# Windowed attention with a gated feed-forward block: the score table added by TensorE in jobs 1 to 12, one reduction for both heads' minima, the first 27 steps' scores in two-bank tiles

## The chip, the cores and the metric

The kernel runs on one core of a Trainium2 chip. Its engines work through queues of their own, each in order: TensorE (PE, with its weight loads shown as PEld), VectorE (DVE), ScalarE (ACT), GpSimd (POOL) and SyncE (SP, which here only issues loads). TensorE writes its results to PSUM, which the program uses as eight banks of 512 fp32 columns; the rest lies in SBUF. The metric is the time of one execution on the device in microseconds, less is better.

## What is computed

Attention over 4 batches, 8 heads, 768 positions and 64 dimensions, where a query sees the last 96 keys and the first 8, with a slope of distance for each head, and then a feed-forward block with a three-tap convolution and a gate:

```python
scores = scale * np.matmul(q, k.transpose(0, 1, 3, 2))
keep = is_global | is_local
slopes = 2.0 ** (-8.0 * (np.arange(H, dtype=np.float32) + 1) / H)
bias = -slopes[:, None, None] * dist[None, :, :]
scores = np.where(keep, scores + bias, -1000000000.0)
a = np.exp(scores - np.max(scores, axis=-1, keepdims=True))
attn = np.matmul(a / (np.sum(a, axis=-1, keepdims=True) + 1e-09), v)
...
h = np.maximum(x @ w_in, 0.0)          # x is attn, heads side by side
conv_out[s] = sum(conv_w[k] * h[s + k - 1] for k in range(3))
out = (h * sigmoid(conv_out)) @ w_out
```

## The kernel before

**Jobs and steps.** A job is one batch, one half of the positions (384) and one pair of heads; there are 32 jobs, numbered m, and each has three steps i of 128 queries. Step s is step i of job m, s = 3m + i, so jobs 1 to 12 are steps 3 to 38. A query block sees a window of 232 key columns (96 before it, its own 128, and 8 global ones); the first block of a batch sees 136.

**What a step does.** `scores` multiplies q by k for both heads into PSUM. In jobs 0 to 8 ("native", `m < NATIVE`) these are plain fp32 matmuls of 64 rows, head 0 in rows 0 to 63 and head 1 in rows 64 to 127 (line 384); head 0's tile is s, head 1's is sb, in different banks. From job 9 on q is split into a high and a low fp32r part (qh, ql) and k is stacked (kk), and each head takes two matmuls (line 394), both heads in one bank. `maxima` is VectorE's: one pass per head over the scores in PSUM adds the bias table `tab` (bf16, a column block per head; masked places hold a huge value), scales by -0.125, writes the result back and keeps the minimum in mm (line 411, in the profile as CUSTOM_DVE_ANT_0 with an accumulator read behind it). `exps` is ScalarE's: exp(minimum - value) for each head into one of three buffers pbuf, with the sum (line 425). `normalise` takes the reciprocal on VectorE (437) and multiplies head 0 on GpSimd (443) and, in the first 40 steps, head 1 on ScalarE (441). Two steps later `transposes` turns both heads on TensorE (451), ScalarE copies them out (453), and at a job's end `values` multiplies by v (469) and `mixed` splits the result into xh and xl (481, 482).

**The feed-forward block.** A half of a batch is four jobs, 12 steps. Then `mm1` (line 500; 521 for the first piece, done early) multiplies by w_in, ScalarE's relu goes to hbuf (510), `conv` runs on GpSimd (546) and VectorE (547, 548), a gate and a check on ScalarE (566, 577), `split` on VectorE and ScalarE (599 to 602), and `mm2` multiplies by w_out (611). These items are spread over the steps of the next half.

**Decode.** The weights arrive as 64-bit floats in 16 pieces (w0_0 to w7_1) and VectorE cuts them into fp32 by three operations a piece (315, 317, 319); GpSimd casts the high plane wih or woh (324) and VectorE subtracts the low plane wil or wol (330). How many such operations are put behind a step's minima is set by budgets in us: `DECODE_BY_HAND` for steps 0 to 10 and `DECODE_LATER` from step 11 on. A piece's load waits until a slot of four is free.

**Loads.** SyncE issues all of them in one order: q and k of a job (rq, rk; line 111 for native jobs, four loads each), v (122) and weight pieces (306). The program lets the issue of a load wait for the landing of the eighth before it. `prep` casts k and q of jobs from 9 on, on GpSimd (136, 137), and VectorE subtracts (140, 141).

**Order.** Steps 0 to 10 stand in the order in which the code is written, with matmuls on zeros (`warm`, 169) between them. From step 11 on a scheduler orders each engine's instructions. PSUM: two buffers of s (a bank each), two of transposes, one of pv, and three others m0 to m2, of which m0 and m1 hold sb up to step 26 and then products of the feed-forward block.

## Time and profile before

| what | us |
|---|---|
| median of three runs | 463.97 |
| lowest and highest of them | 452.75, 464.49 |
| the profiled execution | 452.65 |
| its span, first to last instruction | 450.7 |
| TensorE busy in the span | 434.5 |
| VectorE busy | 351.9 |
| ScalarE busy | 304.0 |
| GpSimd busy | 225.8 |

The busy time of an engine is the union of its instructions; a matmul's end is modelled, so it says when TensorE had something in flight, not that it ran at its peak. A view by windows gives these times for a stretch, with the number of instructions in brackets, TensorE's granted clock (1.00 is 2.4 GHz), and the share of time in which the DMA engines were busy. The chain of waits goes back from the last instruction to what released it, and so on to the start: what stands in it set the time.

### The profile page before, as it was taken

Reading aid. Unit: us, or ns where it says so; the run is one execution under the profiler, and the core shown is the slowest. Engines: PE = TensorE matmul, PEld = TensorE weight load, DVE = VectorE, ACT = ScalarE, POOL = GpSimd, SP = SyncE. Lnnn points to the kernel's source line nnn. Section 1 sums busy time; section 2 is a strip of 40 time slices with the busy share of each in tenths; the row PEclk is TensorE's granted clock in tenths of the full one; section 3 lists DMA queues with packets and bytes.
Section 4 is the critical chain, followed back from the end, with each engine's and each line's share of the span. In section 5 each row is a group of like instructions: output and inputs, shape, how many; then the busy total and the mean of one; then the engine's idle time right before and its main releaser. Section 6 shows DMA issues by size and latency. Waiting matters only on the chain.

```text
span 450.7 us, 9020 instructions
## 1 busy us (share of the span) xinstructions
PE 434.5 (96%) x3027; PEld 375.6 (83%) x3027; DVE 351.9 (78%) x927; ACT 304.0 (67%) x839; POOL 225.8 (50%) x315
## 2 busy tenths in 40 slices
PE   8789999999889999999999999999999999998997
PEld 6555678899768988899989988889989988798876
DVE  6899998889989877757989897847989986447800
ACT  3778878788799667647776576646775696547610
POOL 5654446637835472656675585646675651022000
PEclk9989999999999999999999999999999999999999
DMA  6979941343244332353234333442335223584111
GB/s 213 306 221 275 279 121 43 108 147 105 83 129 150 108 107 97 92 166 107 86 120 160 107 108 91 130 138 81 106 119 163 81 83 119 207 293 132 47 49 52
DMA packets 22662, 60.02 MB, mean 133 GB/s; under 512 B 3024, under 2 KB 5584, under 8 KB 22608
## 3 DMA queue, kind: packets, MB, share of 16 engines
q1 hardware_dynamic: 18992, 53.01, 38.1%
q10 hardware_dynamic: 3616, 6.36, 3.8%
q8 instruction: 26, 0.43, 0.4%
q14 instruction: 28, 0.23, 0.2%
HBM read 53.07 MB, written 6.29 MB: 132 GB/s over the span
## 4 chain that ended last, share of the span: by engine, by line
PE 73%; DVE 5%; ACT 4%; DMA 4%; POOL 2%; issue 2%; ACTq 0%; POOLq 0%; DVEq 0%
PE o L611 24%; PE h L500 24%; PE pv L469 7%; PE t L451 7%; PE s L394 6%; DMA check<-in_w 3%; DVE c L547 1%; PE last L632 1%; POOL pbuf L443 1%; PE sb L384 1%; PE s L384 1%; DVE c L548 1%; DVE c L599 1%; ACT pbuf L425 1%; ACT sat L577 1%
## 5 line engine op out<-in xcount | busy, mean ns | idle before, releaser
L443 POOL TENSOR_SCALAR pbuf<-pbuf,mm 128x232 f32<-128x232 f32 (+1 forms) x152 | 109.1, 726 | 74.1 <-DVE mm L437 49.2
L425 ACT ACTIVATE pbuf<-s,mm 128x232 f32<-128x232 f32 (+1 forms) x165 | 72.5, 444 | 37.6 <-DVE mm L411 22.8
L411 DVE CUSTOM_DVE_ANT_0 s<-s,tab 128x232 f32<-128x232 f32 (+1 forms) x165 | 63.1, 384 | 24.9 <-PE s L394 21.8
L546 POOL TENSOR_SCALAR c<-hbuf,cw 128x382 f32<-128x382 f32 (+1 forms) x64 | 50.0, 786 | 59.3 <-ACT hbuf L510 59.3
L611 PE MATMUL o<-woh,gh 128*128 128x512 f32 x184 | 74.0, 402 | 0.0
L611 PE MATMUL o<-wol,gh 128*128 128x512 f32 x184 | 73.2, 398 | 0.0
L611 PE MATMUL o<-woh,gl 128*128 128x512 f32 x184 | 73.2, 399 | 0.0
L451 PE MATMUL t<-ident,pbuf 128*128 128x128 f32 x384 | 63.0, 278 | 6.6 <-ACT pbuf L441 3.7
L453 ACT ACTIVATE pt<-t 128x512 f32<-128x512 f32 x96 | 58.0, 604 | 15.4 <-PE t L451 15.3
L451 PEld LDWEIGHTS t<-ident,pbuf 128*128 128x128 f32 x384 | 45.5, 141 | 19.6 <-ACT pbuf L441 5.1
L500 PE MATMUL h<-xh,wih 128*128 128x384 f32 x252 | 58.1, 345 | 1.7 <-ACT hbuf L510 1.2
L500 PE MATMUL h<-xl,wih 128*128 128x384 f32 x252 | 58.8, 342 | 0.0
L500 PE MATMUL h<-xh,wil 128*128 128x384 f32 x252 | 56.3, 340 | 0.0
L469 PE MATMUL pv<-pt,v 128*64 128x128 f32 (+1 forms) x768 | 50.0, 279 | 0.3 <-ACT pt L453 0.3
L469 PEld LDWEIGHTS pv<-pt,v 128*64 128x64 f32 (+1 forms) x768 | 42.3, 138 | 8.9 <-issue 2.5
L500 PEld LDWEIGHTS h<-xh,wih 128*128 128x128 f32 x252 | 42.9, 189 | 4.1 <-ACT hbuf L510 1.9
L547 DVE SCALAR_TENSOR_TENSOR c<-hbuf,cw,c 128x382 f32<-128x382 f32 (+1 forms) x64 | 43.7, 697 | 3.0 <-POOL c L546 2.7
L500 PEld LDWEIGHTS h<-xh,wil 128*128 128x128 f32 x252 | 44.2, 189 | 0.3 <-issue 0.3
L500 PEld LDWEIGHTS h<-xl,wih 128*128 128x128 f32 x252 | 44.0, 189 | 0.2 <-issue 0.2
L548 DVE SCALAR_TENSOR_TENSOR c<-hbuf,cw,c 128x382 f32<-128x382 f32 (+1 forms) x64 | 43.4, 686 | 0.3
L510 ACT ACTIVATE hbuf<-h 128x384 f32<-128x384 f32 x64 | 31.9, 500 | 17.4 <-PE h L500 17.0
L611 PEld LDWEIGHTS o<-woh,gl 128*128 128x128 f32 x184 | 34.7, 188 | 7.7 <-issue 0.2
(119 smaller groups left out, 846.6 us busy)
## 6 DMA issues: line engine op xcount, KB each, us to landing
v<-in_vv SPq DMA_DIRECT2D x32, 384.0 KB, 3.7
rq<-in_qk SPq DMA_DIRECT2D x23, 384.0 KB, 3.1
wr<-in_w SPq DMA_DIRECT2D x16, 512.0 KB, 5.2
check<-in_w SPq DMA_DIRECT2D x16, 512.0 KB, 4.6
rk<-in_qk SPq DMA_DIRECT2D x12, 504.0 KB, 3.6
out<-ob ACTq DMA_DIRECT2D x23, 256.0 KB, 2.1
rk<-in_qk SPq DMA_DIRECT2D x11, 408.0 KB, 3.2
rq<-in_qk SPq DMA_DIRECT2D x16, 96.0 KB, 4.4
```

The source lines that it names most:

```text
L411: last_ttr[s] = V.tensor_tensor_reduce(out=sp[j][:, c0 : c0 + n], in0=sp[j][:, c0 : c0 + n], in1=tb, scale=-0.125, scalar=3.0e38, op0=ALU. ...
L425: last_exp[s] = A.activation(pb[:, j, c0 : c0 + n], sp[j][:, c0 : c0 + n], AF.Exp, bias=mm[:, j : j + 1], scale=-1.0, accum_out=mm[:, 2 + ...
L443: G.tensor_scalar(x, x, inv, 1.0, ALU.mult, ALU.mult)
L451: T.transpose(pt[:, j, c, :], pb[:, j, c * P : (c + 1) * P], ident)
L453: last_ev[s] = A.activation(sb, pt, AF.Copy)
L469: T.matmul(pv[m][64 * j : 64 * j + 64, i * P : (i + 1) * P], vt[m][:n, i, c, 64 * j : 64 * j + 64], sb[:n, j, c, :], start=c == 0, stop=c ...
L500: T.matmul(ps[:, :TB], w_[:, k, fs], x_, start=part == 0 and k == 0, stop=part == 2 and k == NK - 1,)
L510: A.activation(half, ps[:, :TB], AF.Relu, scale=0.5)
L546: G.tensor_scalar(c, *tap(1), 1.0, ALU.mult, ALU.mult)
L547: V.scalar_tensor_tensor(c, *tap(0), c, ALU.mult, ALU.add)
L548: V.scalar_tensor_tensor(c, *tap(2), c, ALU.mult, ALU.add)
L611: last = T.matmul(ps, g_[:, f], w_[:, f], start=f == 0 and part == 0, stop=f == NF - 1 and part == 2,)
```

## The change

For jobs 1 to 12 the table is no longer added by VectorE. q is scaled by -0.125 (native jobs: in place, 384 columns, by GpSimd, one multiplication per job, placed where job m - 1 begins; jobs 9 to 12: in the cast and the subtraction that were there). TensorE adds the table with one more matmul per head into the same PSUM columns: the weights are `ident16`, a bf16 identity times -0.125, made once by ScalarE, and the moving data is the table itself, 232 or 136 columns. VectorE then takes the minima of both heads with one `tensor_reduce` and writes nothing back.

For the first 27 steps the scores of both heads lie in one tile of two banks, with two buffers, in place of s and sb. At step 27 this pool is closed, and its four banks become two buffers of s and the banks m0 and m1. The decode budgets are raised. Steps 0 to 2 and 39 to 95 compute as before.

```diff
+BIASED = (1, 13)
-DECODE_BY_HAND, DECODE_LATER = (0.3, 1.2, 1.4), (1.2, 1.2)
+DECODE_BY_HAND, DECODE_LATER = (0.3, 1.5, 1.8), (1.6, 1.6)
...
     def prep(m, part):
+        if m < NATIVE and biased(m) and part == 0:
+            q = raw[m][0][:, :TB]
+            G.tensor_scalar(q, q, -0.125, 1.0, ALU.mult, ALU.mult)
         if m >= len(jobs) or m < NATIVE:
             return
...
-            G.tensor_copy(qh, rq)
+            if biased(m):
+                G.tensor_scalar(qh, rq, -0.125, 1.0, ALU.mult, ALU.mult)
+            else:
+                G.tensor_copy(qh, rq)
...
+            if biased(m):
+                V.scalar_tensor_tensor(ql, rq, -0.125, qh.bitcast(F32), ALU.mult, ALU.subtract)
+            else:
+                V.tensor_tensor(ql, rq, qh.bitcast(F32), ALU.subtract)
...
     table(1, WIN, X=A)
+    A.activation(ident16, ident, AF.Copy, scale=-0.125)
...
-        both = ps_s.tile([P, 2, 256], F32, tag="s", name=f"s{s}")
-        sp = [both[:, 0], bank(f"sb{s}", True) if m < BESIDE else both[:, 1]]
+        if m < BESIDE:
+            both = wide[1].tile([P, 2, 512], F32, tag="s", name=f"s{s}")
+        else:
+            if not ps_s:
+                narrow()
+            both = ps_s[0].tile([P, 2, 256], F32, tag="s", name=f"s{s}", bufs=2)
+        sp = [both[:, 0], both[:, 1]]
+
+        def bias(j):
+            last_mm[s] = T.matmul(
+                sp[j][:, c0 : c0 + n], ident16, bias_of(s, j), start=False, stop=True
+            )
...
+            if biased(m):
+                bias(j)
+        for j in range(2 if m < NATIVE and biased(m) else 0):
+            bias(j)
...
+        if biased(m):
+            last_ttr[s] = V.tensor_reduce(
+                mm[:, 0:2], both[:, :, c0 : c0 + n], axis=mybir.AxisListType.X, op=ALU.min,
+            )
+        for j in range(0 if biased(m) else 2):
             last_ttr[s] = V.tensor_tensor_reduce(
```

What it does to the order is shown in two places. The first is TensorE around steps 15 and 16 (t11 to t13 are transposes of steps 11 to 13, h0_0 the first product of the feed-forward block, pv3 the values of job 3). Before:

```order
L384 MATMUL s15_760<-rk5_585,rq5_586 128x232
L521 MATMUL h0_0_665<-xl1_623,wih_186 128x384
L521 MATMUL h0_0_665<-xh1_622,wil_187 128x384
L384 MATMUL sb15_761<-rk5_585,rq5_586 128x232
L451 MATMUL t11_724<-ident_153,pbuf2_195 128x128 x4
L521 MATMUL h0_0_665<-xh2_717,wih_186 128x384
L384 MATMUL s16_814<-rk5_585,rq5_586 128x232
L451 MATMUL t12_749<-ident_153,pbuf0_193 128x128 x4
L384 MATMUL sb16_815<-rk5_585,rq5_586 128x232
```

And in the changed program:

```order
L417 MATMUL s15_784<-rk5_594,rq5_595 128x232 x2
L409 LDWEIGHTS ident16_158
L409 MATMUL s15_784<-tab_167,ident16_158 128x232
L409 LDWEIGHTS ident16_158
L409 MATMUL s15_784<-tab_167,ident16_158 128x232
L567 MATMUL h0_0_680<-xh2_734,wih_188 128x384
L567 MATMUL h0_0_680<-xl2_735,wih_188 128x384
L567 MATMUL h0_0_680<-xh2_734,wil_189 128x384
```

The two heads' scores, which other work parted before, now stand side by side, with the two additions behind them.

The second place is GpSimd between the normalisations (pbuf) of steps 13 and 16 or 17; c0 is the convolution, woh a cast of weights. Before:

```order
L443 TENSOR_SCALAR pbuf1_194<-pbuf1_194,mm13_711 128x232
L324 CAST woh_188<-w4_1_756 128x512
L443 TENSOR_SCALAR pbuf2_195<-pbuf2_195,mm14_740 128x232
L443 TENSOR_SCALAR pbuf0_193<-pbuf0_193,mm15_764 128x232
L546 TENSOR_SCALAR c0_879<-hbuf_190,cw_185 128x382
L324 CAST woh_188<-w5_0_803 128x512
L443 TENSOR_SCALAR pbuf1_194<-pbuf1_194,mm16_818 128x232
```

And in the changed program:

```order
L489 TENSOR_SCALAR pbuf1_196<-pbuf1_196,mm13_729 128x232
L346 CAST woh_190<-w5_0_749 128x512
L141 TENSOR_SCALAR rq7_831<-rq7_831 128x384
L489 TENSOR_SCALAR pbuf2_197<-pbuf2_197,mm14_758 128x232
L489 TENSOR_SCALAR pbuf0_195<-pbuf0_195,mm15_789 128x232
L592 TENSOR_SCALAR c0_903<-hbuf_192,cw_187 128x382
L141 TENSOR_SCALAR rq8_968<-rq8_968 128x384
L346 CAST woh_190<-w5_1_776 128x512
L346 CAST woh_190<-w6_0_823 128x512
L489 TENSOR_SCALAR pbuf1_196<-pbuf1_196,mm16_843 128x232
```

The casts have moved forward by one or two pieces, and the scaling of q for jobs 7 and 8 stands between the normalisations.

## Rows read from the trace of the kernel before

**Rows 1.** The page's first lines: the span, and TensorE's busy time.

```profile
span 450.7 us, 9020 instructions
...
PE 434.5 (96%) x3027; PEld 375.6 (83%) x3027; DVE 351.9 (78%) x927; ACT 304.0 (67%) x839; POOL 225.8 (50%) x315
```

**Rows 2.** Windows over all engines. After each stretch and its length: PE, PEld, DVE, ACT and POOL busy us with instructions, the granted clock, the DMA engines' busy share, GB/s.

```profile
10.00:35.00 25.00, 20.07 (x175) 14.20 (x175) 23.29 (x84) 18.79 (x65) 15.94 (x23) 0.93 0.89 271
35.00:84.00 49.00, 47.98 (x331) 36.05 (x330) 46.39 (x133) 39.10 (x127) 26.36 (x36) 1.00 0.62 181
84.00:98.00 14.00, 13.53 (x103) 12.44 (x102) 11.21 (x30) 11.56 (x35) 7.32 (x9) 1.00 0.36 122
98.00:140.00 42.00, 38.37 (x286) 33.07 (x285) 38.98 (x84) 35.82 (x101) 23.67 (x24) 1.00 0.34 106
...
200.00:400.00 200.00, 200.00 (x1410) 179.00 (x1407) 157.30 (x404) 133.19 (x354) 108.57 (x143) 1.00 0.39 123
```

**Rows 3.** Pieces of the chain of waits in order of time: start, length, what.

```profile
69.73 2.29 PE h L500 x12
...
100.69 3.13 DMA rq<-in_qk
...
105.69 1.41 POOL pbuf L443
...
118.88 2.61 DVE c L547 x3
...
413.41 22.39 PE o L611 x96
```

**Rows 4.** Windows for line 411 alone (VectorE's minima): its busy time, instructions, clock, DMA share, GB/s.

```profile
10.00:35.00 25.00, 7.28 (x40) 0.93 0.89 271
35.00:84.00 49.00, 13.11 (x60) 1.00 0.62 181
98.00:140.00 42.00, 7.90 (x36) 1.00 0.34 106
```

**Rows 5.** Groups of instructions by line and shape: line, engine, operation, out<-in, count, then busy us, mean ns, idle before. Two shapes of the minima, the subtraction of `mixed`, which reads 384 columns of PSUM, and, from the page, the exponential.

```profile
L411 DVE CUSTOM_DVE_ANT_0 s<-s,tab 128x232 f32<-128x232 f32 x138 | 55.1, 401 | 19.6 <-PE s L394 16.9 <-POOL tab L227 1.2 <-ACT sat L577 0.4
...
L482 DVE TENSOR_TENSOR xl<-pv,xh 128x384 fp32r<-128x384 f32 x32 | 17.6, 551 | 1.6 <-ACT xh L481 1.3
...
L411 DVE CUSTOM_DVE_ANT_0 s<-s,tab 128x136 f32<-128x136 f32 x27 | 8.1, 299 | 5.3 <-PE s L394 4.8 <-PE sb L384 0.3
...
L425 ACT ACTIVATE pbuf<-s,mm 128x232 f32<-128x232 f32 (+1 forms) x165 | 72.5, 444 | 37.6 <-DVE mm L411 22.8
```

**Rows 6.** The timeline of TensorE in the hand-written part, step 5: start, length, operation. Each head's fp32 matmul runs in two parts.

```profile
16.80 0.46 PE L384 MATMUL s<-rk,rq 64*128 64x232 f32 x1
16.81 0.46 PE L384 MATMUL sb<-rk,rq 64*128 64x232 f32 x1
17.11 0.36 PE L384 MATMUL s<-rk,rq 64*128 64x232 f32 x1
...
17.40 0.44 PE L451 MATMUL t<-ident,pbuf 128*128 128x128 f32 x2
```

**Rows 7.** The same timeline in the scheduled part, one step of job 5; x2 are the two parts of one head.

```profile
48.55 0.66 PE L384 MATMUL s<-rk,rq 64*128 64x232 f32 x2
49.14 0.66 PE L451 MATMUL t<-ident,pbuf 128*128 128x128 f32 x4
49.73 0.66 PE L384 MATMUL sb<-rk,rq 64*128 64x232 f32 x2
50.31 0.44 PE L521 MATMUL h<-xh,wih 128*128 128x384 f32 x1
```

**Rows 8.** Windows for line 384 alone (native scores, steps 12 to 26): PE and PEld busy.

```profile
35.00:84.00 49.00, 16.43 (x60) 8.13 (x60) 1.00 0.62 181
```

**Rows 9.** Two pieces of the chain of waits: four score matmuls of 232 columns (two heads, high and low part) of jobs from 9 on, each with its own weights.

```profile
96.08 0.40 PE s L394 x4
...
147.91 0.65 PE s L394 x4
```

**Rows 10.** GpSimd's groups by line and shape: a multiplication by a constant over 368 columns.

```profile
L227 POOL TENSOR_SCALAR tab<-setup 128x368 bf16<-128x368 f32 x6 | 3.8, 649 | 0.2
```

**Rows 11.** The timeline of VectorE: the first decode operation of a piece at two times.

```profile
16.77 0.71 DVE L315 TENSOR_SCALAR w<-wr 128x512 int32<-128x512 int32 x1
...
45.10 0.43 DVE L315 TENSOR_SCALAR w<-wr 128x512 int32<-128x512 int32 x1
```

**Rows 12.** The timeline of GpSimd; in square brackets the idle time before an instruction and what ended it.

```profile
43.85 0.46 POOL L443 TENSOR_SCALAR pbuf<-pbuf,mm 128x232 f32<-128x232 f32 x1
47.72 1.07 POOL L324 CAST woh<-w 128x512 fp32r<-128x512 f32 x1 [3.42 <-DVE w L319]
...
52.50 0.65 POOL L546 TENSOR_SCALAR c<-hbuf,cw 128x382 f32<-128x382 f32 x1 [2.40 <-ACT hbuf L510]
...
54.13 0.63 POOL L443 TENSOR_SCALAR pbuf<-pbuf,mm 128x232 f32<-128x232 f32 x1
```

**Rows 13.** SyncE's timeline at two issues of q loads (the last half of job 7's, both halves of job 8's), and from the view of loads their size and the median time from issue to landing.

```profile
42.92 0.47 SPq L111 DMA_DIRECT2D rq<-in_qk  x1
...
51.98 1.11 SPq L111 DMA_DIRECT2D rq<-in_qk  x2
...
rq<-in_qk SPq DMA_DIRECT2D x16, 96.0 KB, 4.4
```

More of the change, by code (lines that the diff above doesn't have):

```diff
@@ L82, in fast_path, with narrow @@
     pg = pool("pg", 4)
-    ps_s = pool("ps_s", 2, space=PSUM)
     ps_t = pool("ps_t", 2, space=PSUM)
     ps_v = pool("ps_v", 1, space=PSUM)
-    ps_m = pool("ps_m", 1, space=PSUM)
+    ps_m = {2: pool("ps_m", 1, space=PSUM)}
     p2 = pool("p2", 2)
+    ps_w = tc.tile_pool(name="ps_w", bufs=2, space=PSUM)
+    wide = [ps_w, ps_w.__enter__()]
+    ps_s = []
+    def narrow():
+        wide[0].__exit__(None, None, None)
+        ps = tc.tile_pool(name="ps_s", bufs=1, space=PSUM)
+        ps_s.append(ps.__enter__())
+        ps_m[0] = ps_m[1] = ps_s[0]
+        pools.insert(len(pools) - 1, ps)
     jobs = [(b, u, hp) for b in range(B) for u in range(2) for hp in range(NPAIR)]
@@ L123, in load_v, with biased @@
         vt[m] = t
+    def biased(m):
+        return BIASED[0] <= m < BIASED[1]
     def prep(m, part):
+        if m < NATIVE and biased(m) and part == 0:
+            q = raw[m][0][:, :TB]
+            G.tensor_scalar(q, q, -0.125, 1.0, ALU.mult, ALU.mult)
         if m >= len(jobs) or m < NATIVE:
@@ L140, in prep @@
             V.tensor_tensor(kk[64:], rk[64:], kk[64:].bitcast(F32), ALU.subtract)
-            V.tensor_tensor(ql, rq, qh.bitcast(F32), ALU.subtract)
+            if biased(m):
+                V.scalar_tensor_tensor(ql, rq, -0.125, qh.bitcast(F32), ALU.mult, ALU.subtract)
+            else:
+                V.tensor_tensor(ql, rq, qh.bitcast(F32), ALU.subtract)
     manual = tc.manual_schedule()
@@ L151, in fast_path, with bank @@
     load(1)
-    turns = [0, 0]
-    def bank(name, scores=False):
+    turns = [0]
+    def bank(name):
         s = cur.get("s", 0)
         own = (2,) if s < NB * BESIDE else (0,) if exact else (0, 1, 2)
-        if scores:
-            own = (0, 1)
-        turns[scores] += 1
-        k = own[turns[scores] % len(own)]
-        return ps_m.tile([P, 512], F32, tag=f"m{k}", name=name)
+        turns[0] += 1
+        k = own[turns[0] % len(own)]
+        return ps_m[k].tile([P, 512], F32, tag=f"m{k}", name=name)
     queue, cur, exact = [], {}, []
@@ L192, in fast_path @@
     make_identity(nc, ident)
+    ident16 = const.tile([P, P], BF16, name="ident16")
     V.tensor_copy(rel, reli)
@@ L388, in scores @@
                     start=True,
-                    stop=True,
+                    stop=not biased(m),
                 )
@@ L392, in scores @@
             qh, ql, kk = qk[m]
-            for n_, (q_, st, sp_) in enumerate(((qh, True, False), (ql, False, True))):
+            for n_, (q_, st, sp_) in enumerate(((qh, True, False), (ql, False, not biased(m)))):
                 last_mm[s] = T.matmul(
@@ L400, in scores, with bias_of @@
                 )
-        st_s[s] = (sp, c0, n, first)
+            if biased(m):
+                bias(j)
+        for j in range(2 if m < NATIVE and biased(m) else 0):
+            bias(j)
+        st_s[s] = (sp, c0, n, both)
+    def bias_of(s, j):
+        m, i = steps[s]
+        b, u, hp = jobs[m]
+        if u == 0 and i == 0:
+            return tab[:, 2 * hp + j, WIN:]
+        return tab[:, 2 * hp + j, 0:WIN]
     def maxima(s):
@@ L405, in maxima @@
         b, u, hp = jobs[m]
-        sp, c0, n, first = st_s[s]
+        sp, c0, n, both = st_s[s]
         mm = p1.tile([P, 8], F32, tag="mm", name=f"mm{s}", bufs=6)
-        for j in range(2):
-            h = 2 * hp + j
-            tb = tab[:, h, WIN:] if first else tab[:, h, 0:WIN]
+        if biased(m):
[3 more added lines that the diff above has]
+        for j in range(0 if biased(m) else 2):
             last_ttr[s] = V.tensor_tensor_reduce(
-                out=sp[j][:, c0 : c0 + n], in0=sp[j][:, c0 : c0 + n], in1=tb,
+                out=sp[j][:, c0 : c0 + n], in0=sp[j][:, c0 : c0 + n], in1=bias_of(s, j),
                 scale=-0.125, scalar=3.0e38, op0=ALU.add, op1=ALU.min,
@@ L957, in general_head @@
         for c, (a, z) in enumerate(parts):
-            sp = ps_s.tile([P, 512], F32, tag="s", name=f"gs{t}_{c}")
+            sp = ps_s[0].tile([P, 512], F32, tag="s", name=f"gs{t}_{c}", bufs=2)
             T.matmul(
```

## Prediction

> **What bounds the kernel now.** I read the page's summary first, then the windows by stage, then the chain of waits. The summary has a span of 450.7 us, in which TensorE shows as 96% busy [rows 1]; the profiled execution took 452.65 us, so 1.95 us lie around the span. That execution equals the lowest of the three runs shown (452.75) and is 2.4% under their median of 463.97; my sum is made against 452.65, and my time is for an execution like it.
>
> The windows split the span [rows 2]. From 200 to 400 us TensorE is busy without a hole, and the chain there and to the end is made of TensorE's own matmuls, such as the 96 of the output product in one piece of 22.39 us [rows 3]. Nothing of the change touches that part. Ahead of it stand three stages, which I name A (10 to 35 us, steps 3 to 11, by hand), B (35 to 84 us, steps 12 to 26) and C (84 to 140 us, steps 27 to 38). VectorE is busy 23.3 of 25 us in A, 46.4 of 49 in B, 11.2 of 14 and 39.0 of 42 in C; TensorE 20.1, 48.0, 13.5 and 38.4 [rows 2]. So in A VectorE is the tightest, in B both are full, and in C VectorE leads again with ScalarE and GpSimd close by. The chain says the same: TensorE's pieces in B, then at 100 us a load of rq, a multiplication of GpSimd, and convolution steps of VectorE [rows 3]. All 36 changed steps lie in A, B and C, so what is won must be won there, and later stages keep it.
>
> **VectorE: two passes become one.** In B the line of the minima takes 13.11 us for 60 instructions, which is 15 steps of two passes and two accumulator reads: 0.874 us a step; in A it is 0.728 (10 steps, some of them narrow), in C 0.878 [rows 4]. A reduction over 2 x 232 columns of PSUM stands nowhere in the trace. The pass takes 401 ns for 232 columns and 299 ns for 136 [rows 5], so 1.06 ns a column and 155 ns beside it; 464 columns give 647 ns, and 272 give 443 ns. Bounds: not under the 551 ns of the 384-column read of PSUM, which is shorter work [rows 5], and not over two passes, 802 ns. I take 647, since the 384-column row falls on the same line (562 worked out, 551 seen). A wide step so saves 0.23 us (0.07 to 0.32). A and B together have 24 such steps, some narrow in A: 9 x 0.2 + 15 x 0.23 = 5.3 us of VectorE's time. C has 12: 2.7 us.
>
> The larger decode budgets add no work. They bring weight steps forward: by the pass of step 12 five more of them are done, and the last plane of w7_1 comes right ahead of the pass of step 21 or 22 in place of step 27. What A saves on the minima it spends on these, so A alone gets no shorter; B gets it back. I count A and B together for this reason.
>
> **TensorE: the table is added, and split pairs are joined.** In the hand-written part the two heads' scores run beside each other: s and sb start at 16.80 and 16.81, and the transposes follow at 17.40, so 0.60 us for both [rows 6]. In B the scheduler has pulled them apart: s at 48.55, transposes at 49.14, sb at 49.73, the next product at 50.31; each head alone takes the same 0.59 us [rows 7]. The order of the changed program has both heads in one row (x2) in every step of B, then the two additions. By the window, native scores hold TensorE 16.43 us in B, 1.10 us a step [rows 8]; at 0.60 that is 9.0, so 7.4 us go. Each addition is a matmul of 232 columns with its own weight load. The nearest rows are the four 232-column score matmuls of later jobs, 0.40 us in one piece and 0.65 in another, so 0.10 to 0.16 us each [rows 9]. The 30 additions of B cost 3.0 to 4.8 us, and B's net for TensorE is 2.6 to 4.4 us less. In A 18 additions cost 1.8 to 2.9 us; TensorE idles 4.9 us of A and runs warming matmuls besides, which hides them. In C 24 additions cost 2.4 to 3.8 us, with no pair to join; TensorE idles 0.5 + 3.6 us there, which covers them only if they fall into holes. Without that cover C would be up to 3.8 us longer.
>
> **GpSimd: eight more multiplications in its queue.** Jobs 1 to 8 get q scaled in place, 384 columns each; the nearest row is 368 columns at 649 ns [rows 10], so 5.2 us in all. The rows of the trace range either way: VectorE's 512-column bit step takes 0.71 us at 16.77 and 0.43 us at 45.10 [rows 11], so an operation can stretch by 0.28 us, depending on what runs beside it. GpSimd is busy 15.9 of 25 us in A and 26.4 of 49 in B [rows 2], so the time itself fits. What matters is where they stand. GpSimd works in order, and behind a multiplication that waits for its load stand the casts of weights and the normalisations of older steps. Jobs 9 to 12 multiply where they cast, and subtract with a scale where they subtracted: same sizes, no price taken. The scaled identity is one small ScalarE operation ahead of its first exponential, free: ScalarE waits there for the first minimum.
>
> **Waits added.** Scores of a native job now wait for GpSimd besides the load; both stand two steps ahead of their use. The one minimum waits for both heads and the additions, about 0.2 to 0.3 us later, and the first exponential for it; VectorE has decode steps to do meanwhile. Two banks are freed together, after the second exponential in place of the first, so an exponential's 0.44 us later for one head [rows 5].
>
> **The sum.** A and B: VectorE gives 5.3 us, TensorE in B 2.6 to 4.4; since both are full there, the smaller decides, and I take 3.7. C: VectorE gives 2.7, TensorE takes 2.4 to 3.8 in holes of 4.1; I take half of VectorE's, 1.3. Loads, transposes and everything after 140 us: 0. 452.65 - 3.7 - 1.3 = 447.65, say 447.7 us. With the bounds, the gain runs from 0 (each step saves 0.07 us, 1.7 us in A and B, and additions in C take it back) to about 9 (4.4 in B, 1.5 in A, 3 in C), so 443.5 to 452.7.
>
> **Rivals.**
> *Slower: GpSimd is held up at a load.* In the changed order q of job 8 is scaled right behind the first convolution step, ahead of two casts and the normalisation of step 16. Before, that place in the queue was reached at 53.15 (52.50 + 0.65) [rows 12]; the two loads of rq8 were issued in 1.11 us from 51.98 on and such a load lands after 4.4 us [rows 13], so 56.4 to 57.0: 3.2 to 3.8 us with GpSimd idle. For q of job 7 the last load was issued at 42.92, to land at 47.3, and a 512 KB weight load now stands ahead of it, 1.9 us at the 271 GB/s of A [rows 2]: 49.2. The queue is free for it from 44.3 on, but before it waited until 47.72 for a decode step anyway [rows 12], so 1.5 us are new; job 5 the same, 1.5. If all 6.5 us end in transposes that come late, with three buffers between them and the exponentials, A and B lose 6.5 and win nothing, C still wins 1.3: 457.9 us. Against it: the transposes of step 16 stand about two steps (6 us) further back in the changed order. It decides from about 3.7 us of such lateness on, where it eats the gain of A and B.
> *No gain: the loads set the pace.* The DMA engines are 0.89 busy in A [rows 2]. If steps come sooner but loads do not, B begins as before and TensorE waits instead: only C's 1.3 us and a bit, 450.3 to 453.5, middle 452.
> *Multiplications beside decode steps.* Eight more GpSimd operations of 0.65 us each stretch a decode step by between the 0.28 us of [rows 11] and their own length: 2.2 to 5.2 us of VectorE's time in A and B, off the 5.3. Then A and B win between 3.1 and 0.1: 448.3 to 451.3 with C's share, 450 in the middle. The Trainium skill speaks for this one (SBUF — State Buffer, Who interferes with whom): a VectorE instruction with two SBUF inputs contends with a GpSimd instruction that reads SBUF, and the loser blocks for the whole instruction. By that rule the time would be near 450. The stretch at 16.77 agrees in kind; the trace cannot show how often it will happen. The same section says that a reduction never contends, which leaves the 647 ns alone.
> *More than the sum.* If A and B give VectorE's whole 5.3 us and C its whole 2.7, because the joined pairs leave TensorE room, it is 8.0 us: 444.6, and with the 1.0 us in which TensorE is idle in B [rows 2] 443.6.
>
> **Chances and range.** Forecast (446 to 449.5) 0.45; multiplications beside decode (449.5 to 451.5) 0.16; loads set the pace (to 453.5) 0.13; GpSimd held up, slower than before (453.5 to 459) 0.13; more than the sum 0.13. The range 443.5 to 459 leaves out about one in ten at the two ends and takes in the bounds above; the forecast's own is 446 to 449.5. A measurement of this kernel can tell about 2% from no change. Faster by that means under 443.6: the outer part of the last case, and 0.10 in all. Slower means over 461.7, beyond the held-up case: 0.05. The rest, 0.85, is within 2%.
>
> **What would show it.** Right: one reduction a step of 0.6 to 0.7 us; additions at 0.10 to 0.16; native scores near 9 us in B; step 27 reached 3 to 5 us earlier; the same stretch from there to the end less about 1.3. Wrong: GpSimd idle over 2 us ahead of a scaled q with TensorE waiting on its normalisations; a reduction near 0.8 us; or stage C longer than before by more than 2 us, which would mean that the additions are on the path there.

## The result

The changed kernel takes 455.77 us, median of 6 runs (455.39 to 456.26). Against the runs of the kernel before near 452.6 us (the 464 of the median shown ahead belongs to executions in a slower state, which every comparison here leaves out) the ratio is 1.0062, 95% interval 1.0045 to 1.0080: 2.8 us slower. The forecast was 447.7, about 5 us faster. The time lies in the range, on the wrong side of no change.

The page of the changed kernel, first lines, to be read against [rows 1]:

```profile
span 453.9 us, 9089 instructions
...
PE 435.9 (96%) x3099; PEld 378.0 (83%) x3099; DVE 351.2 (77%) x819; ACT 303.7 (67%) x840; POOL 237.0 (52%) x323
```

TensorE's busy sum did not fall, it rose by 1.4 us, and the time around it by 1.8. The windows of the stages, columns as in [rows 2]:

```profile
10.00:35.00 25.00, 19.24 (x174) 14.04 (x174) 23.29 (x55) 16.62 (x57) 17.59 (x26) 0.86 0.90 271
35.00:84.00 49.00, 45.08 (x364) 33.86 (x361) 45.06 (x90) 39.53 (x129) 30.80 (x39) 1.00 0.58 174
84.00:98.00 14.00, 12.66 (x103) 10.74 (x102) 9.34 (x19) 12.51 (x41) 6.72 (x10) 1.00 0.29 87
98.00:140.00 42.00, 41.78 (x309) 37.51 (x311) 36.88 (x59) 34.18 (x96) 21.77 (x24) 1.00 0.37 113
```

In B TensorE now stands idle for 3.9 us where it was 1.0, in A for 5.8 where it was 4.9; at the start of C (84 to 98 us) it is 1.3 and was 0.5, and in the long part of C the 3.6 us of idle time are gone (0.2 left). By the start of the minima of each step, step 8 comes 1.0 us later than before, step 12 4.4, step 19 8.7 and step 27 6.0; from step 57 on every step is 3.0 us late. So A and B lose. How much C gives back depends on the row that one takes: by the first exponential of each step the delay is 3.4 us at step 27 and 3.0 at step 39, with swings of 3 us either way between them.

The single prices of the forecast, windows for one line each: the reduction (VectorE), then the native scores and the additions (TensorE).

```profile
35.00:84.00 49.00, 9.84 (x16) 1.00 0.58 174
```

```profile
35.00:84.00 49.00, 10.14 (x64) 4.64 (x60) 1.00 0.58 174
```

```profile
35.00:84.00 49.00, 5.88 (x32) 1.82 (x32) 1.00 0.58 174
84.00:140.00 56.00, 6.69 (x26) 2.41 (x26) 1.00 0.35 107
```

0.615 us a reduction and 10.14 us for 16 steps of native scores (9.5 for 15, forecast 9.0) are close to what the forecast had. The additions, 0.18 to 0.26 us each by busy time, include ends that overlap the next instruction.

The waits between 10 and 84 us, sum, times, longest:

```profile
POOL rq L141 <- DMA rq<-in_qk: 8.5, 3, 3.6
...
PE t L497 <- POOL pbuf L489: 5.5, 5, 2.2
```

The three waits of GpSimd stand ahead of q of jobs 3, 6 and 8 (1.99, 3.60 and 2.87 us); of these the slower rival had named job 8 alone. GpSimd's timeline at the first of them, and TensorE's behind it:

```profile
25.12 0.86 POOL L141 TENSOR_SCALAR rq<-rq 128x384 f32<-128x384 f32 x1 [1.99 <-DMA rq<-in_qk]
...
26.69 0.94 POOL L141 TENSOR_SCALAR rq<-rq 128x384 f32<-128x384 f32 x1
27.62 0.80 POOL L489 TENSOR_SCALAR pbuf<-pbuf,mm 128x136 f32<-128x136 f32 x1
```

```profile
28.47 1.12 PE L497 MATMUL t<-ident,pbuf 128*128 128x128 f32 x4 [2.23 <-POOL pbuf L489]
...
31.04 2.83 PE L515 MATMUL pv<-pt,v 128*64 128x128 f32 x24
...
42.24 1.54 PE L515 MATMUL pv<-pt,v 128*64 128x128 f32 x24
```

A normalisation stands behind two multiplications of q, the transposes wait 2.23 us for it, and after that hole the clock is low: the 24 products of pv take 2.83 us at 31.04 and 1.54 at 42.24. It looked as if this rival were the whole story. The experiments say that it is not.

### The profile page after: what moved, and what is told of

Read it like the earlier page. It is cut to its first block, busy times and chain, and to the rows that moved or that the text cites. A ratio compares the mean times of both kernels' runs of the same rounds, so it can differ in the third digit from the quotient of the medians.

```text
span 453.9 us, 9089 instructions
## 1 busy us (share of the span) xinstructions
PE 435.9 (96%) x3099; PEld 378.0 (83%) x3099; DVE 351.2 (77%) x819; ACT 303.7 (67%) x840; POOL 237.0 (52%) x323
## 3 DMA queue, kind: packets, MB, share of 16 engines
q1 hardware_dynamic: 18992, 53.01, 37.5%
## 4 chain that ended last, share of the span: by engine, by line
PE 63%; DMA 3%; DVE 1%; ACT 1%; issue 0%; ACTq 0%; DVEq 0%; SPq 0%
PE o L657 24%; PE h L546 20%; PE pv L515 6%; PE t L497 6%; PE s L427 6%; DMA check<-in_w 3%; PE last L678 1%; ACT junkb L371 0%; DVE junk L367 0%; DVE c L594 0%; DVE c L593 0%; ACT sat L623 0%; ACT olast L690 0%; ACT hbuf L556 0%; ACTq L665 0%
## 5 line engine op out<-in xcount | busy, mean ns | idle before, releaser
L489 POOL TENSOR_SCALAR pbuf<-pbuf,mm 128x232 f32<-128x232 f32 (+1 forms) x152 | 115.2, 767 | 73.8 <-DVE mm L483 48.0
L471 ACT ACTIVATE pbuf<-s,mm 128x232 f32<-128x232 f32 (+1 forms) x192 | 83.7, 444 | 39.8 <-DVE mm L457 30.5
L497 PEld LDWEIGHTS t<-ident,pbuf 128*128 128x128 f32 x384 | 46.7, 141 | 19.6 <-POOL pbuf L489 8.2
L457 DVE CUSTOM_DVE_ANT_0 s<-s,tab 128x232 f32<-128x232 f32 (+1 forms) x120 | 46.3, 388 | 18.6 <-PE s L427 16.2
L593 DVE SCALAR_TENSOR_TENSOR c<-hbuf,cw,c 128x382 f32<-128x382 f32 (+1 forms) x64 | 45.2, 717 | 5.3 <-POOL c L592 5.0
L594 DVE SCALAR_TENSOR_TENSOR c<-hbuf,cw,c 128x382 f32<-128x382 f32 (+1 forms) x64 | 44.5, 704 | 0.4
```

The lines of the kernel that those rows point to most:

```text
L457: last_ttr[s] = V.tensor_tensor_reduce(out=sp[j][:, c0 : c0 + n], in0=sp[j][:, c0 : c0 + n], in1=bias_of(s, j), scale=-0.125, scalar=3.0e3 ...
L471: last_exp[s] = A.activation(pb[:, j, c0 : c0 + n], sp[j][:, c0 : c0 + n], AF.Exp, bias=mm[:, j : j + 1], scale=-1.0, accum_out=mm[:, 2 + ...
L489: G.tensor_scalar(x, x, inv, 1.0, ALU.mult, ALU.mult)
L497: T.transpose(pt[:, j, c, :], pb[:, j, c * P : (c + 1) * P], ident)
L593: V.scalar_tensor_tensor(c, *tap(0), c, ALU.mult, ALU.add)
L594: V.scalar_tensor_tensor(c, *tap(2), c, ALU.mult, ALU.add)
```

## The experiments

Ratios are to runs of the kernel before, made beside each kernel; "before" below is that kernel, and 1% of it is 4.5 us. Its own median differed from round to round (452.2 to 454.3 us), so kernels of different rounds are compared by their ratios and not by their times. A difference of two ratios is uncertain by the root of the summed squares of their intervals. Edits are against the changed kernel unless said otherwise.

**First round: is it the queue, or the budgets?** `e1_q_unscaled`:

```
-            G.tensor_scalar(q, q, -0.125, 1.0, ALU.mult, ALU.mult)
...
-    A.activation(ident16, ident, AF.Copy, scale=-0.125)
+    A.activation(ident16, ident, AF.Copy)
...
-                ... op=ALU.min)
+                ... op=ALU.max)
+            V.tensor_scalar(mm[:, 0:2], mm[:, 0:2], -0.125, None, ALU.mult)
```

> Edit: no q is scaled, neither in GpSimd's queue for jobs 1 to 8 nor in the casts of jobs 9 to 12; the table is added with an unscaled identity, the reduction takes the maximum, a 128x2 VectorE operation multiplies it by -0.125, and the exponential scales by 0.125. All else as in the changed kernel. Theory Q (GpSimd, in order, is held at a q whose load has not landed, and the normalisations behind it come late): GpSimd's waits for a load of q (8.5 us in three pieces between 20 and 66 us) are gone, TensorE's transposes no longer wait for GpSimd 5.5 + 7.5 us in 10 to 84 us, and the time falls from 455.8 by 4 to 8 us, to 448 to 452, with some 1 us lost to 36 small VectorE operations. Theory D (the larger decode budgets put more decode work ahead of the minima of the hand-written steps 8 to 10): no gain, 455 to 457. Theory T (the additions and the heads tied together cost TensorE what they save): no gain, 455 to 457.

Measured: 458.52 us, ratio 1.0120 (1.0088 to 1.0153). No gain, a loss. The waits for q are gone, and other holes stand in their place:

```profile
PE s L408 <- ACT pbuf L463: 4.8, 4, 1.6
...
PE t L489 <- POOL pbuf L481: 2.3, 3, 1.5
```

This run does not price the queue alone: in each of 36 steps it also puts a VectorE operation between the minimum and the exponential, 0.23 us long and 5.8 us in all from start to start, and the last two runs below show that added work of VectorE is paid for. So it shows only that the change without these waits is no gain, not what the waits cost.

`e2_q_later`, the scaling written at the second step of the job before (`if i == 1` in place of `i == 0`):

> Edit: the scaling of q for jobs 1 to 8 stays on GpSimd, but is written one step later (second step of the job before, instead of the first), behind one more normalisation; all else as in the changed kernel. Theory Q: the loads have some 2.5 to 3 us more, so most of the 8.5 us of GpSimd's waits for loads of q are gone and the normalisation behind each is not late: 455.8 falls by 2 to 6 us, to 450 to 454. Theory D and theory T: 455 to 457, as nothing else moves.

Measured: 459.31, ratio 1.0135 (1.0089 to 1.0180). The edit did not do what it was for: GpSimd still waited 9.0 us for loads of q, so this run says little.

`e3_old_budgets`:

```
-DECODE_BY_HAND, DECODE_LATER = (0.3, 1.5, 1.8), (1.6, 1.6)
+DECODE_BY_HAND, DECODE_LATER = (0.3, 1.2, 1.4), (1.2, 1.2)
```

> Edit: the changed kernel with the decode budgets of the kernel before, (0.3, 1.2, 1.4) and (1.2, 1.2). Theory D: steps 8 to 11, which start 1.0 to 4.1 us later than before the change, start as before, and the time falls by about 3 us or more, to 450 to 453. Theory Q: GpSimd still waits at the loads of q; the time stays within 1.5 us of 455.8, or gets longer where the decode of the first weights is late. Theory T: the same as Q.

Measured: 457.97, ratio 1.0119 (1.0080 to 1.0157). Steps 9 to 18 came earlier than in the changed kernel (step 18 by 4.2 us), and a hole at the end of B took it back: the product at 86.97 waits 3.8 us for an eviction of h on ScalarE. (The profiled execution, 455.56 us, is the fastest of six.)

```profile
PE h L546 <- ACT hbuf L556: 3.8, 1, 3.8
```

`e4_before_times_one`, the kernel before with `G.tensor_scalar(q, q, 1.0, 1.0, ALU.mult, ALU.mult)` in `prep`:

> Edit: the kernel before, with GpSimd multiplying q of jobs 1 to 8 by 1.0 in place, at the place where the changed kernel scales it; the scores, two passes of minima, banks and budgets are those of before. Theory Q: the queue place alone costs what the change lost and what it did not win, 452.6 becomes 456 to 460, with GpSimd waiting at loads of q in pieces of over 2 us and transposes waiting for it. Theories D and T: the multiplications fit in GpSimd's idle time, 452 to 453.5.

Measured: 453.98, ratio 1.0035 (1.0001 to 1.0068): some 1.6 us, with GpSimd waiting 6.1 us for loads and TensorE 4.1 us for GpSimd. The queue place costs something in the kernel before, far less than its waits.

**Second round: one part at a time.** `e5_two_bank_tiles_only`, the changed kernel with `BIASED = (0, 0)` and the old budgets:

> Edit: of the change only the two-bank tiles are kept: no step is biased (no scaled q, no additions, two fused passes a step), and the decode budgets are those of before. So the two heads' native scores stand together, which in the changed kernel took TensorE 15.8 us of issue time for all 27 steps against 24.2 before. Theory T (TensorE bounds the whole, and in the change the additions cost it what the joined pairs save): the saving stands alone here, 452.6 - 4 to 8 = 445 to 449. Theory H (TensorE's holes: a step's chain from its scores to its transposes sets the pace, and two heads tied to one tile make it longer): TensorE idles instead, 452 to 457.

Measured: 455.03, ratio 1.0050 (1.0035 to 1.0066). Its page, its window of B, and TensorE's wait between 35 and 84 us (0.8 before):

```profile
span 452.0 us, 9024 instructions
...
PE 429.0 (95%) x3027; PEld 373.4 (83%) x3027; DVE 355.0 (79%) x927; ACT 304.7 (67%) x840; POOL 226.8 (50%) x315
```

```profile
35.00:84.00 49.00, 43.44 (x332) 33.65 (x330) 47.53 (x136) 39.90 (x129) 29.92 (x36) 0.97 0.62 184
```

```profile
PE s L417 <- ACT pbuf L471: 4.2, 6, 1.1
```

The pairs are joined and TensorE's busy sum is 5.5 us lower than in [rows 1], where the forecast counts on 7.4 in B; the span is 1.3 us longer, so 6.8 us of holes came in. VectorE is busy 47.5 of 49 us there. One caution: with both heads in one tile the second pass waits for the first (0.49 us between their starts in the hand-written steps, 0.32 before), so this run also costs VectorE some 0.17 us a step.

`e6_no_additions`, the call of `T.matmul` in `bias` left out:

> Edit: the changed kernel without the 72 additions; the distance table is left out of the scores of jobs 1 to 12, all else (scaled q, one reduction, two-bank tiles, budgets) stays. Theory T: the additions' 7 to 11 us of TensorE are gone in full, 445 to 449. Theory H: only part of it is seen, since TensorE's holes in A and B (9.7 us in 10 to 84 us) stay or grow, 451 to 455.

Measured: 452.72, ratio 1.0000 (0.9986 to 1.0015): all 72 additions are worth 2.8 us here, 0.04 each, and even without them nothing is won. They are not what A and B lose: by the first exponential of step 27 this run is 4.1 us later than before, the changed kernel 3.4.

`e7_native_jobs_only`, `BIASED = (1, 9)`, and `e8_later_jobs_only`, `BIASED = (9, 13)`:

> Edit: only jobs 1 to 8 are biased; jobs 9 to 12 have their two fused passes back and no additions. Theory T: stage C gets back the 3.6 us of holes that it had, and TensorE loses 24 additions there, at 0.26 us each by the windows of the changed kernel; the two cancel within 1.5 us of 455.8 unless TensorE is late there, in which case 451 to 454. Theory H: the loss of A and B stays and the gain of C is lost, 456 to 460.

> Edit: only jobs 9 to 12 are biased; jobs 0 to 8 have two fused passes a step and no scaled q, but keep the two-bank tiles and the larger budgets. Theory T: joined pairs without additions in A and B, 446 to 450. Theory H with its cause in the additions and the scaled q: A and B as before the change and C's holes filled, 448 to 451; with its cause in the tiles or the budgets: 455 or more.

Measured: 456.02, ratio 1.0064 (1.0037 to 1.0090), and 457.37, ratio 1.0101 (1.0085 to 1.0117). The tiles and the larger budgets without any scaled q or addition in A and B lose as well, which no version of "the additions or q alone" explains; the changed kernel, which has both on top of them, is 1.8 us faster than e8 (uncertain by 1.1). And without jobs 9 to 12 (e7) the change is as slow as with them: what they give, in this kernel, is 0.1 us (uncertain by 1.4).

**Third round: the tie undone.** `e9_heads_untied`:

```
-            both = wide[1].tile([P, 2, 512], F32, tag="s", name=f"s{s}")
+            both = None
+            sp = [wide[1].tile([P, 512], F32, tag=f"s{j}", name=f"s{j}_{s}") for j in range(2)]
...
+        for j in range(2 if biased(m) and both is None else 0):
+            last_ttr[s] = V.tensor_reduce(mm[:, j : j + 1], sp[j][:, c0 : c0 + n], ... op=ALU.min)
```

> Edit: the changed kernel, but in steps 0 to 26 each head keeps a tile of one bank, two buffers per head as before, and the minima are two tensor_reduces of one head each instead of one over both. Scaled q, additions, larger budgets and all of jobs 9 to 12 as in the changed kernel. Theory K (the loss is the tie: two heads in one tile can only be begun together and are freed together, so TensorE stands idle at native scores where it took up other work before): 452 to 454, with fewer waits of native scores for exponentials. Theory A (the additions and what waits for them are the loss, as leaving them out gave 3.1 us back): 455 to 458, as all 72 additions are there. Theory Q (the scaled q in GpSimd's queue): also 455 to 458.

Measured: 465.29, ratio 1.0223 (1.0194 to 1.0252). The theory of the tie (K) falls: undone, the loss is more than three times as large. With the additions and the larger budgets around them, the two-bank tiles and the single reduction that goes with them save 7.3 us.

`e10_before_new_budgets`:

> Edit: the kernel before with the larger decode budgets (0.3, 1.5, 1.8) and (1.6, 1.6), nothing else. Theory D (the budgets delay the minima): 455 to 458. Theories K, A and Q: within 1 us of before, 452 to 453.5.

Measured: 456.72, ratio 1.0053 (1.0032 to 1.0074), 2.4 us slower. The budgets, which the forecast had at nothing, cost that in the kernel before.

`e11_untied_later_jobs_only`, the edit of e9 with `BIASED = (9, 13)` and the old budgets:

> Edit: jobs 0 to 8 as in the kernel before (a bank per head, two fused passes, no scaled q, old budgets); only jobs 9 to 12 are biased, with their additions, scaled casts and single reduction. Theory K: A and B as before, C's 3.6 us of TensorE's holes filled by the additions, so 451 to 453.5. Theory A: the 24 additions of C (0.26 us each in the changed kernel) are more than its holes, 454 to 457.

Measured: 451.20, ratio 0.9938 (0.9914 to 0.9963): 2.8 us faster than before and, by the ratios, 5.6 faster than the changed kernel. This version beats both. Its windows of A and C beside [rows 2], the busy times of its page, and its additions in C:

```profile
10.00:35.00 25.00, 19.43 (x178) 13.52 (x179) 23.25 (x84) 19.66 (x69) 15.91 (x22) 1.00 0.90 272
...
98.00:140.00 42.00, 40.92 (x298) 36.53 (x297) 39.65 (x62) 36.98 (x101) 22.83 (x24) 1.00 0.32 104
```

```profile
PE 433.8 (97%) x3051; PEld 375.9 (84%) x3051; DVE 352.4 (79%) x891; ACT 304.6 (68%) x840; POOL 229.7 (51%) x315
```

```profile
84.00:140.00 56.00, 6.29 (x24) 2.30 (x24) 1.00 0.37 116
```

By their starts (from an addition to the next matmul) those 24 take 1.37 us, 0.04 each in most cases. That is not their whole price, as e16 below shows: the product behind an addition starts the next one 0.08 us later than it does behind a score. TensorE's idle time in C goes from 3.6 to 1.1 us. Not all of the gain is C's: this execution's span is 1.9 us shorter, and by the first exponentials it is 0.8 to 0.9 us ahead from step 12 to step 23 already, before any changed step, with a granted clock of 1.00 in A where [rows 2] has 0.93. So about 1.0 us of the 1.9 comes from C on.

`e12_heads_untied_old_budgets`:

> Edit: as the run with the heads untied, and the decode budgets of before. Theory K: 452 to 454. Theory D: lower than the run with the heads untied by 2 us or more. Theory A and Q: 455 to 458.

Measured: 459.99, ratio 1.0125 (1.0098 to 1.0152). K falls again; with the heads parted the larger budgets cost 4.4 us (e9 against this run).

**Fourth round: what stands between e11 and e12.** `e14_untied_no_native_additions` leaves out, of e12, the additions of jobs 1 to 8; `e15_untied_q_unscaled` leaves out their scaled q:

> Edit: the run with the heads untied and old budgets (460.0 us) without the additions of jobs 1 to 8; the distance table is left out of their scores, all else stays. Theory S: with the heads parted TensorE is full in A and B, and 48 additions at some 0.2 us each stand on its path: 450 to 452. Theory Q (the scaled q in GpSimd's queue is the loss): 457 to 460.

> Edit: the run with the heads untied and old budgets (460.0 us), but q of jobs 1 to 8 is not scaled on GpSimd: the table is added with an unscaled identity, the reductions take maxima, a 128x2 VectorE operation multiplies them by -0.125 and the exponential scales by 0.125 there. Theory S: TensorE's additions are all there, 458 to 461. Theory Q: 452 to 455.

Measured: 452.52, ratio 1.0003 (0.9976 to 1.0029), and 457.93, ratio 1.0129 (1.0096 to 1.0162). The 48 additions of A and B cost 5.5 us by the ratios (uncertain by 1.7), 0.11 us each. Leaving q unscaled wins nothing (0.2 us more, uncertain by 1.9), but as in e1 a VectorE operation stands in its place, in 24 steps, so what the scaled q costs here stays open. Pages of e12 and of e14:

```profile
span 459.8 us, 9098 instructions
...
PE 443.9 (97%) x3099; PEld 382.3 (83%) x3099; DVE 352.8 (77%) x843; ACT 304.3 (66%) x840; POOL 230.6 (50%) x323
```

```profile
span 450.9 us, 9004 instructions
...
PE 436.0 (97%) x3051; PEld 378.7 (84%) x3051; DVE 353.0 (78%) x843; ACT 303.9 (67%) x840; POOL 234.1 (52%) x323
```

The span differs by 8.9 us and TensorE's busy sum by 7.9 (e12's profiled execution is the slowest of its six): here the additions are on the path. TensorE's timeline of e12 shows native scores with the heads parted:

```profile
50.80 0.66 PE L418 MATMUL s<-rk,rq 64*128 64x232 f32 x2
51.39 0.27 PE L410 MATMUL s<-tab,ident 128*128 128x232 bf16 x1
51.59 0.66 PE L418 MATMUL s<-rk,rq 64*128 64x232 f32 x2
...
52.97 0.27 PE L410 MATMUL s<-tab,ident 128*128 128x232 bf16 x1
53.01 0.42 PE L572 MATMUL h<-xh,wih 128*128 128x384 f32 x1
```

Each head takes 0.59 us, and an addition 0.20 when another native score follows (51.39 to 51.59) and 0.04 when a product of h does (52.97 to 53.01). What an addition costs depends on its neighbour.

`e13_tiles_and_later_jobs` (e11 with the two-bank tiles) and `e16_jobs_9_to_24` (e11 with `BIASED = (9, 25)`):

> Edit: as the run with only jobs 9 to 12 biased and the heads untied (451.2 us), but with the two-bank tiles in jobs 0 to 8; old budgets, two fused passes and no scaled q there. Theory S (TensorE and VectorE are both nearly full in A and B, so relieving TensorE alone by the joined pairs gives nothing): 452 to 454.5, TensorE's busy sum some 5 us lower and its holes larger by that and more. Theory of the prediction (TensorE's saving counts): 445 to 448.

> Edit: as the run with only jobs 9 to 12 biased and the heads untied (451.2 us), with jobs 13 to 24 biased as well, which lie after 140 us where TensorE has no hole. Theory S: each of the 72 further additions costs its 0.04 to 0.06 us of TensorE (1.37 us for 24 by the starts in that run), so 454 to 455.5. If VectorE's saving counted anywhere behind 140 us: 447 to 451.

Measured: 460.55, ratio 1.0183 (1.0155 to 1.0212), and 460.64, ratio 1.0183 (1.0124 to 1.0242). Against e11 the two-bank tiles of e13 cost 11.1 us, far outside both theories. e13 runs within 0.4 us of e5 up to step 24, and then loses at step 27, where the first score in the narrow tiles waits 4.0 us for an exponential and the clock of 84 to 98 us is 0.76:

```profile
84.00:98.00 14.00, 9.79 (x70) 8.88 (x70) 9.32 (x18) 9.56 (x32) 6.10 (x7) 0.76 0.24 80
```

e16 confirms the sign of theory S and not its size: 72 additions where TensorE has no hole cost 11 us by the ratios (uncertain by 2.9) and 9.7 by the spans of the two profiled executions, 0.13 to 0.15 each, and TensorE's busy sum rises from 433.8 to 442.2:

```profile
PE 442.2 (96%) x3123; PEld 382.5 (83%) x3123; DVE 348.4 (76%) x783; ACT 307.1 (67%) x840; POOL 223.1 (49%) x315
```

The expectation had its price, 0.04 to 0.06, from the distance between an addition and the next start. That misses half of it. Scores of later jobs in the kernel before, then in e16:

```profile
150.58 0.28 PE L394 MATMUL s<-kk,ql 128*128 128x232 f32 x1
150.70 0.27 PE L394 MATMUL s<-kk,qh 128*128 128x232 f32 x1
150.81 0.27 PE L394 MATMUL s<-kk,ql 128*128 128x232 f32 x1
```

```profile
161.97 0.27 PE L428 MATMUL s<-kk,ql 128*128 128x232 f32 x1
162.08 0.27 PE L410 MATMUL s<-tab,ident 128*128 128x232 bf16 x1
162.12 0.35 PE L428 MATMUL s<-kk,qh 128*128 128x232 f32 x1
162.31 0.27 PE L428 MATMUL s<-kk,ql 128*128 128x232 f32 x1
```

Behind another score a score product takes 0.11 us to the next start (150.70 to 150.81), behind an addition 0.19 (162.12 to 162.31). In the median over e16's run from 140 us on, the products of h (0.26 in place of 0.18) and of o (0.32 in place of 0.24) are late by the same 0.08 us. So an addition costs 0.04 + 0.08 = 0.12 us there, 8.6 us for 72, which is most of what e16 lost.

**Last: the same work on VectorE, twice.** `e17_changed_repeat` and `e18_untied_repeat` add to the changed kernel and to e12:

```
+        if biased(m) and m < NATIVE:
+            V.tensor_reduce(mm[:, 0:1], sp[0][:, c0 : c0 + n], axis=mybir.AxisListType.X, op=ALU.min)
```

> Edit: the changed kernel with one more VectorE reduction in each of the 24 steps of jobs 1 to 8 (the first head's minimum is taken twice, to the same place), some 0.3 us each by the starts, 7.4 us in all; TensorE's work is unchanged. Theory V (with the pairs joined and the reduction, VectorE and the chain through it, not TensorE, set the pace of A and B): 4 to 8 us more, 460 to 464. Theory S (TensorE's sum sets it): 0 to 2 us more, 455.5 to 458.

> Edit: the run with the heads untied and old budgets (460.0 us) with the same 24 repeated minima of the first head, 7.4 us of VectorE. There TensorE has the additions and the parted heads on it, and VectorE was busy for 40.6 of the 49 us of B. Theory V: 4 to 8 us more here too, 464 to 468. Theory S: TensorE is full and VectorE has the room, 0 to 3 us more, 460 to 463.

Measured: 461.67, ratio 1.0178 (1.0113 to 1.0242), and 464.58, ratio 1.0266 (1.0218 to 1.0315). Against their bases that is 1.2% and 1.4%, 5 to 6 us each (uncertain by 3.0 and 2.5), of the 7.4 put in. VectorE's work is paid for in both, so theory S, that TensorE's sum alone sets the pace, falls as well, and the pair of runs does not tell the two kernels apart.

## Why the prediction was wrong

The runs make a ladder from the kernel before to the changed one. By the ratios, with 453 us as the base:

| rung | ratio | us |
|---|---|---|
| before to e11: jobs 9 to 12 | 1 to 0.9938 | -2.8 |
| e11 to e14: scaled q, reductions in place of passes, jobs 1 to 8 | to 1.0003 | +2.9 |
| e14 to e12: their 48 additions | to 1.0125 | +5.5 |
| e12 to e3: two-bank tiles, one reduction | to 1.0119 | -0.3 |
| e3 to changed: larger budgets | to 1.0062 | -2.6 |

The first rung is uncertain by 1.1 us, the others by 1.7 to 2.1, so the fourth is not told from nothing. The last four, which touch steps of A and B, sum to 5.5 us lost. But a rung's price belongs to its place on the ladder. The same runs give a second one, with other culprits: before to e11 -2.8; e11 to e13, the two-bank tiles, +11.1; e13 to e8, the larger budgets, -3.7; e8 to changed, scaled q, additions and reductions of jobs 1 to 8, -1.8. On the first ladder the additions are the loss and the tiles nothing; on the second the tiles are the loss and the additions part of a gain. So no single part is shown to be the cause.

**The step that failed** is the sum of A and B, "since both are full there, the smaller decides, and I take 3.7", and in it TensorE's term: 7.4 us off by the joined pairs, counted as time of the kernel. The pairs did come off TensorE: e5 has its busy sum 5.5 us lower. The time did not follow: e5 is 2.3 us slower, and in B TensorE's idle time goes from 1.0 to 5.6 us while VectorE is busy for 47.5 of 49 us. e6 shows the same with the reduction in place: it has every saving that the forecast counts and no addition to set against them, which by the forecast's own terms is its case of more than the sum, 444.6 us, and its ratio is 1.0000. Removed work became holes. I argue, from the holes of e5, that the time which a parted head took up in [rows 7] was largely time in which TensorE would have waited anyway; which wait stands in its place differs from run to run, and in the changed kernel most of the 9.7 us of holes in A and B end at GpSimd's normalisations (5.5 us) and at ScalarE (3.1).

**The additions** were priced about right (0.11 to 0.13 where they show, forecast 0.10 to 0.16). They were paid for in full after 140 us, where TensorE had no hole (e16), and, with the heads parted, in A and B (48 x 0.10 to 0.16 is 4.8 to 7.7; measured 5.5). The 18 of A, which I had called hidden, are in that: by the first exponential of step 12 e12 is 2.0 us behind e14. In the changed kernel itself, with its holes, all 72 are worth only 2.8 us (e6).

**VectorE** was mis-sized. I compared busy times, 0.874 us for two passes against 0.647. Starts are what count when an engine is full; here are the two passes of one step before, then the reduction after:

```profile
24.11 0.40 DVE L411 CUSTOM_DVE_ANT_0 s<-s,tab 128x232 f32<-128x232 f32 x1
...
24.43 0.44 DVE L411 CUSTOM_DVE_ANT_0 sb<-sb,tab 128x232 f32<-128x232 f32 x1
...
24.78 0.16 DVE L437 RECIPROCAL mm<-mm 128x2 f32<-128x2 f32 x1
```

```profile
37.16 0.64 DVE L453 TENSOR_REDUCE mm<-s 128x2 f32<-128x464 f32 x1
37.71 0.42 DVE L337 TENSOR_SCALAR w<-wr 128x512 int32<-128x512 int32 x1
```

From 24.11 to 24.78 are 0.67 us for the pair, from 37.16 to 37.71 0.55 for the reduction: 0.12 us saved a step, half of the 0.23 in the forecast, 2.9 us in A and B in place of 5.3. The reduction's own 0.63 us was right. VectorE's busy time in the whole span fell by 0.7 us only (351.9 to 351.2), where the forecast had taken off 8.0. With 2.9 in place of 5.3 the rule of the smaller would still have given a gain in A and B, so this size is not what turned the sign.

**Put at nothing in the sum, and not nothing:** the place of q in GpSimd's queue (+1.6 us alone in e4), and the larger budgets (+2.4 us in the kernel before, +4.4 with the heads parted, -2.6 in the changed one). The forecast gave the budgets no price because they add no work; that they move work forward was enough. I named the held-up queue as the slower rival with 6.5 us of waits. Waits of 8.5 us came, ahead of jobs 3, 6 and 8 where the rival had 5, 7 and 8, and TensorE waited 5.5 us for normalisations; but in the kernel before such waits (6.1 us) cost a quarter of their length, and e5 and e8 lose in A and B without any scaled q there (1.8 and 5.7 us by the first exponential of step 27). So that rival is right in what one sees, and not enough to be the cause of the loss; that the time lies in its band, 453.5 to 459, is luck. Its price in the changed kernel was not measured cleanly.

**C, taken alone, was right in sign and near in size:** forecast -1.3; the kernel with that part alone gains 2.8 us (uncertain by 1.1), of which the trace puts about 1.0 of 1.9 into C, as the additions did fall into holes. On top of the rest of the change it gives nothing (e7).

**The other rivals.** Multiplications beside decode steps: over 16 pieces the five groups of decode steps sum to 43.7 us before and 44.8 after, 1.2 us more, not the 2.2 to 5.2 of that rival. By the Trainium skill (SBUF — State Buffer, Who interferes with whom) a VectorE instruction with two SBUF inputs contends with a GpSimd instruction that reads SBUF; that may be behind part of the 1.2 us, which no run here isolates. Loads setting the pace: between 10 and 84 us no wait of TensorE in the changed kernel ends at a load; loads enter only through GpSimd's waits for q. The granted clock, which I had no rival for: it is lower in A (0.86 against 0.93), but e15 has 1.00 throughout and a ratio of 1.0129, and e6, with a mean of 0.984 against 0.992 in the changed kernel, loses nothing; what the low clock of A costs was not measured.

**What stays open.** In A and B extra work on VectorE is paid for, extra work on TensorE is with the heads parted, and work taken off TensorE won nothing in e5 and e6; yet the same joined pairs, with the single reduction, save 7.3 us between e9 and the changed kernel. Five in-order queues meet in every step there. I argue from this that a step's chain runs through both, but this is not shown, and which wait ends last in each step was not settled: the edits also reorder the queues, so parts do not add up (budgets that cost 2.4 us in one kernel win 2.6 in the other, the tiles lose 2.3 us in e5 and 11.1 on top of e11, much of that at the seam of step 27).

## What to carry to other kernels

Where two engines are both nearly full, do not count what is taken off one of them as time until a run shows it; a saving counts where it meets the other engine's hole, as in stage C, and that part alone is the version to keep. Compare replacements on a full engine by the distance between starts and not by busy time, and include the instruction behind, which can start the next one later. Where parts of a change reorder queues, one part's price depends on the others (the two-bank tiles: from 7.3 us won to 11.1 lost), so one ladder of runs is not a proof: look for a second one. And a wait that is plain in the trace is not yet a cost: take it away, with nothing put in its place, and time it before it gets the blame.

## Not expected of the hardware

A 128x232 bf16 addition into PSUM took 0.04 us to the next start ahead of full-height fp32r products (scores of later jobs, h, o), and the product behind it then took 0.08 us longer to its own next start than behind such a score; 0.10 to 0.11 between two additions behind native scores or ahead of transposes, and 0.20 ahead of a score that uses half the rows. A hole of 2.23 us on TensorE ahead of 28.47 was followed by a granted clock of 0.59 from 28 to 35 us, a mean of time at 1.2 and at 2.4 GHz, most of it at the lower; before the change it was 0.85. First the kernel before, then the changed one:

```profile
28.00:35.00 7.00, 6.72 (x55) 5.06 (x55) 6.97 (x26) 4.61 (x18) 4.11 (x5) 0.85 0.82 231
```

```profile
28.00:35.00 7.00, 6.53 (x50) 5.28 (x50) 6.86 (x14) 2.65 (x9) 4.81 (x8) 0.59 0.80 228
```

The busy time of that stretch, 6.53 of 7 us, hides it: TensorE looks nearly full there because its work takes longer.
